# First attention unit loaded in parts, the two heads of a score tile group in turn, and a new order around the start of a fused attention and feed-forward kernel

## The chip, the cores and the metric

The kernel runs on one core of a Trainium2 chip. The metric is the device time of one execution in microseconds (us); the median of several runs is compared. All matrix products run on TensorE (PE), elementwise work on VectorE (DVE) and ScalarE (ACT), a few constants on GpSimd (POOL), and transfers are issued by SyncE (SP) and, in the changed kernel, once by ACT.

## The reference, cut to what matters

```python
def _attn_ref(q, k, v):                       # 4 batches, 8 heads, 576 positions, 64 per head
    scores = scale * np.matmul(q, k.transpose(0, 1, 3, 2))
    mask_local = (rel >= 0) & (rel < 32)                              # heads 0 to 3
    mask_strided = (rel >= 0) & (pos[None, :] % 32 == pos[:, None] % 32)   # heads 4 to 7
    scores = np.where(masks[None], scores, -1e9)
    attn = softmax(scores)                    # exp(s - max) / (sum + 1e-9)
    return np.matmul(attn, v)

x = attn_out as (2304, 512)
x = np.maximum(np.maximum(x @ w1, x @ w2), x @ w3) @ w_out            # 512 -> 768 -> 512
h = x @ w_in                                                          # 512 -> 2048
return (np.maximum(h, 0) + alpha * np.minimum(h, 0)) @ w_out2         # 2048 -> 512
```

Both masks leave only small blocks of the scores: for the local heads 96 queries by 128 keys, for the strided heads (after sorting positions by residue) 108 by 108 or 126 by 126.

## The kernel before

Work on attention comes in units `(b, cc, hf)`: batch `b`, pair of heads `cc` (0 and 1 local, 2 and 3 strided), half `hf`. `ATT_UNITS` gives their order in a batch: (2,0), (2,1), (3,0), (3,1), (0,0), (1,0), (0,1), (1,1). The two heads of a pair lie on partitions 0 to 63 and 64 to 127 of one tile `q` and one tile `k`. A unit has three tiles of each head (two where `cc` is 2 or 3 and `hf` is 1).

For a unit, `scores` (line 325) makes one f32 product per tile and head into two PSUM banks, one per head (tile by tile, head 0 and head 1 in alternation); `masked` (L333, DVE) adds the mask and takes the row extreme; `exponential` (L340, ACT) follows; `reciprocal` (L351, L352) and `normalise` (L364 on DVE or L362 on ACT) come after all of the unit's exponentials; `transposes` (L372, PE) and a copy to `pt` (L264, ACT or DVE) turn each head; `values` (L397, PE) multiplies by v; the result is split into a high and a low part of `x` (L264, L267). Each f32 product shows as two records of PE in the trace.

The feed-forward products of a batch (`L585`, "gates", twelve products of 288 columns for each, and `L607`) need the `x` of all four head pairs of a half, and weights that arrive as 8-byte floats (`raw`, L442), are rebuilt as words by ACT (L456) and DVE (L460, L462) and split into a high part (`w`, L264, ACT) and a low part (L267, DVE).

The order of all this is not written out: each piece is a task with an engine, a cost, and a position `pos`, and `Weave.plan` puts the tasks in order by its own costs, the positions and the rings of buffers. Every engine then runs its list in that order. `first` and `last` set the positions over which a batch's attention is spread; batch 0 stands at -32 to -8, before the first gate at position 0, batch 1 at 16 to 41, among the gates of batch 0. `load_task` issues q and k in one task and v in another, one position later. Two pairs of q and k fit at a time.

`unread` (L214) issues products of 512 columns whose result nobody reads, `WARM` = 6 of them at the start and more as the table `UNREAD` says, so that PE has work while it waits. They read `ident_r`, which POOL makes (L194).

After attention and the first feed-forward part of batches 0 to 2, the last batch and the second feed-forward part follow in an order that the change doesn't touch.

Of the kernel before, what the change touches and what calls it, by code (L numbers as in the profile page):

```python
# [10 lines left out]
F32 = mybir.dt.float32  # L11
F32R = mybir.dt.float32r
# [4 lines left out]
B, H, S, D = 4, 8, 576, 64  # L17
# [4 lines left out]
P = 128  # L22
STRIDE = 32
NA = S // STRIDE
# [6 lines left out]
RG = [(0, 6), (6, 6), (12, 6), (18, 7), (25, 7)]  # L31
# [4 lines left out]
BIG = -8.0e9  # L36
SCALE = 1.0 / math.sqrt(D)
WARM = 6
UNREAD = {((0, 2, 0), 0): 4, ((0, 3, 0), 1): 3, ((0, 1, 0), 0): 9}


NUNITS = 2 * (3 * NF1 + NCC)
NOW = 9
NG = 3 * NF1 // 2
NP = 3
X_SPLIT = 10


class Weave:
# [16 lines left out]
    def add(self, engines, emit, pos, needs=(), gives=(), makes=(), uses=(), mode=None, slack=0):  # L66
        t = len(self.tasks)
        if engines[0][0] != "PE" and any(key in self.banks for key in uses):
            pos -= self.URGENT
        self.banks.update(key for ring, key in makes if ring == "bank")  # L70
        self.tasks.append((engines, emit, pos, needs, makes, mode, slack))
        for ring, key in makes:
            if ring in self.order:
                self.order[ring].append(key)
        for e in gives:
            self.givers.setdefault(e, []).append(t)
            if e[0] == "stored":
                self.stores.add(t)
        for key in [key for _, key in makes] + list(uses):
            self.users.setdefault(key, []).append(t)  # L80
# [84 lines left out]
def attention_maxout_prelu_kernel(  # L165
# [13 lines left out]
    nc = tc.nc  # L179
# [2 lines left out]

    const = ctx.enter_context(tc.tile_pool(name="const", bufs=1, side="left"))
    ident = const.tile([P, P], F32, name="ident")
    ident_r = const.tile([P, P], F32R, name="ident_r")
    mask_l = const.tile([QT, KT], F32, name="mask_l")
    mask_l0 = const.tile([QT, KT], F32, name="mask_l0")
    mask_s = const.tile([P, 126], F32, name="mask_s")
# [1 line left out]

    def build_constants():
        g = nc.gpsimd
        make_identity(nc, ident)
        g.tensor_copy(ident_r, ident)  # L194
        unread(bank(), WARM)
        for m in (mask_l0, mask_l):
            g.memset(m, 0.0)
            g.affine_select(out=m, in_=m, compare_op=ALU.is_ge, fill=BIG, base=32,
                            pattern=[[-1, KT]], channel_multiplier=1)
            g.affine_select(out=m, in_=m, compare_op=ALU.is_ge, fill=BIG, base=-1,  # L200
                            pattern=[[1, KT]], channel_multiplier=-1)
        g.affine_select(out=mask_l0, in_=mask_l0, compare_op=ALU.is_ge, fill=BIG, base=-32,
                        pattern=[[1, KT]], channel_multiplier=0)
        g.memset(mask_s, 0.0)
        ms = mask_s.rearrange("p (r a) -> p r a", a=NA)
        g.affine_select(out=ms, in_=ms, compare_op=ALU.is_ge, fill=BIG, base=0,
                        pattern=[[-NA, 7], [-1, NA]], channel_multiplier=1)
        g.affine_select(out=ms, in_=ms, compare_op=ALU.is_ge, fill=BIG, base=NA - 1,
                        pattern=[[NA, 7], [0, NA]], channel_multiplier=-1)

    def unread(to, n):

        for _ in range(n):
            nc.tensor.matmul(to.rearrange("p (r n) -> p r n", n=P), ident_r,  # L214
                             ident_r.unsqueeze(1).to_broadcast([P, 4, P]), start=True, stop=True)

    def split(hi, lo, src, hi_engine, lo_engine):
        if hi_engine is nc.scalar:
# [26 lines left out]
    qkp = pool(ax, "qkp", 2)  # L245
# [9 lines left out]
    def bank():  # L255
        return ps.tile([P, 512], F32, tag="bank", name="bank")
# [4 lines left out]
    add, tl = weave.add, {}  # L261
# [10 lines left out]
    def dve(n, ops=1):  # L272
        return ("DVE", ops * (75 + 21 * n // 20))

    def load(kb):
        return (("SP", 3 * kb),)
# [13 lines left out]
    def load_task(b, cc, pos):  # L290
        qk, vk = ("q", b, cc), ("v", b, cc)

        def emit_qk(_):
            q = qkp.tile([P, S], F32, tag="q", name="q")
            nc.sync.dma_start(q, qT[b, cc])
            k = qkp.tile([P, S + 32 * (cc < 2)], F32, tag="k", name="k")
            nc.sync.dma_start(k, kTl[b, cc] if cc < 2 else kTs[b, cc - 2])
            tl[qk] = q, k

        def emit_v(_):  # L300
            v = tl[vk] = vp.tile([P, 6 if cc < 2 else 5, 2, D], F32, tag="v", name="v")
            nc.sync.dma_start(v, vl[b, cc] if cc < 2 else vs[b, cc - 2])

        add(load(592), emit_qk, pos, gives=[qk], makes=[("q", qk)])
        add(load(350), emit_v, pos + 1, gives=[vk], makes=[("v", vk)])

    def attention_tasks(b, cc, hf, pos, step):

        u = (b, cc, hf)
        nq, nk, tiles = geometry(cc, hf)  # L310
        n = len(tiles)
        slack = 1500 if b else 0
        ek, qk, vk = ("e", u), ("q", b, cc), ("v", b, cc)
        banks = [("sc", u, j) for j in range(2)]

        def scores(_):
            q, k = tl[qk]
            sc = tl["sc", u] = [bank() for _ in range(2)]
            tl[ek] = ep.tile([P, 2, 3, KT], F32, tag="e", name="e")
            for name in ("nm", "sm", "rc"):  # L320
                tl[name, u] = smp.tile([P, 2, 3], F32, tag=name, name=name)
            for i, (qo, ko, _, _) in enumerate(tiles):
                for j in range(2):
                    rows = slice(D * j, D * (j + 1))
                    nc.tensor.matmul(sc[j][:nq, KT * i:KT * i + nk], q[rows, qo:qo + nq],  # L325
                                     k[rows, ko:ko + nk], start=True, stop=True)

        add((("PE", 2 * n * nk),), scores, pos, needs=[qk], gives=[("sc", u)],
            makes=[("bank", key) for key in banks] + [("e", ek)], uses=[qk], mode="scores")
        for i, (_, _, _, m) in enumerate(tiles):  # L330
            def masked(_, i=i, m=m):
                for j in range(2):
                    nc.vector.tensor_tensor_reduce(  # L333
                        out=tl[ek][:nq, j, i, :nk], in0=tl["sc", u][j][:nq, KT * i:KT * i + nk],
                        in1=m[:nq, :nk], scale=-SCALE, scalar=3.0e38, op0=ALU.add, op1=ALU.min,
                        accum_out=tl["nm", u][:nq, j, i:i + 1])

            def exponential(_, i=i):
                for j in range(2):
                    nc.scalar.activation(tl[ek][:nq, j, i, :nk], tl[ek][:nq, j, i, :nk], AF.Exp,  # L340
                                         bias=tl["nm", u][:nq, j, i:i + 1], scale=-1.0,
                                         accum_out=tl["sm", u][:nq, j, i:i + 1])

            add((dve(nk, 2),), masked, pos, needs=[("sc", u)], gives=[("nm", u, i)],
                uses=banks + [ek])
            add((("ACT", 750),), exponential, pos, needs=[("nm", u, i)], gives=[("exp", u)],
                uses=[ek])

        def reciprocal(_):
# [5 lines left out]
        for j in range(2):  # L355
# [11 lines left out]
            def transposes(_, j=j, trk=trk, ptk=ptk):  # L367
                tr = tl[trk] = bank()
                unread(tr, UNREAD.get((u, j), 0))
                tl[ptk] = ptp.tile([P, 3 * KT], F32, tag="pt", name="pt")  # L370
# [4 lines left out]
            def keep(e, trk=trk, ptk=ptk):  # L375
# [3 lines left out]
                gives=[("nrm", u, j)], uses=[ek])  # L379
            add((("PE", 95 * n),), transposes, pos + step, needs=[("nrm", u, j)], gives=[trk],  # L380
                makes=[("bank", trk), ("pt", ptk)], uses=[ek], mode="transposes", slack=slack)
            add((act(n * nq, True), dve(n * nq)), keep, pos + step, needs=[trk], gives=[ptk],
                uses=[trk, ptk])
# [6 lines left out]
        def values(_):  # L390
# [11 lines left out]
            needs=[vk] + [("pt", u, j) for j in range(2)] + ([begun] if cc >= 2 and hf else []),  # L402
            gives=[pvk] + ([begun] if cc >= 2 and not hf else []), makes=[("bank", pvk)] + [("x", k) for k in fresh],
            uses=[vk] + [("pt", u, j) for j in range(2)] + xks, mode="values", slack=slack)
# [10 lines left out]
        for h in halves:  # L415
# [3 lines left out]
                needs=[pvk], gives=[hik], uses=[pvk])  # L419
# [4 lines left out]
    ATT_UNITS = [(2, 0), (2, 1), (3, 0), (3, 1), (0, 0), (1, 0), (0, 1), (1, 1)]  # L424
# [264 lines left out]
    def last_net(b):  # L689
# [3 lines left out]
        def load_factors(k):  # L693
            if k < NG:
                for i in range(2):
                    t = words["s", k, i] = hw.tile([P, 2, DM], F32R, tag="w", name="w")
                    nc.sync.dma_start(t.bitcast(F32), sd[k - NP][i][:, :, :])
            else:
                n, i = divmod(k - NG, 2)
                load_h(n, ((0, 2), (1, 3))[i])  # L700
# [193 lines left out]
    homes = [("gate", f, g) for f in range(NF1) for g in range(3)] + [("mix", f) for f in range(NF1)]  # L894
    build_constants()
    for b in range(B):
        first, last = (-32, -8) if b == 0 else ((b - 1) * NUNITS + (16 if b == 1 else 3), b * NUNITS - 3)
        step = (last - first) / (len(ATT_UNITS) + 2)
        for i, (cc, hf) in enumerate(ATT_UNITS):
            if i in (0, 2, 4, 5):  # L900
                load_task(b, cc, first + step * i - 8)
            attention_tasks(b, cc, hf, first + step * i, step)
# [35 lines left out]
    for n, _ in enumerate(last_net(B - 1)):  # L938
# [11 lines left out]
        if n == gates - 5:  # L950
            rows = [load_x2(0, 0, xsp, "xs"), load_x2(0, 1, xst, "xst")]
# [329 lines left out]
    for n in range(NQ * NBLK):  # L1281
        blk, q = divmod(n, NQ)
# [68 lines left out]
```

## Time and profile before

| what | value |
|---|---|
| median of 3 runs | 747.61 us (747.39 to 748.48) |
| the profiled execution | 746.98 us, of which the span of the trace is 745.2 us |
| PE, DVE, ACT busy | 99%, 86%, 62% of the span |
| TensorE clock granted, mean of the span | 0.998 of full speed |

The span runs from the first to the last instruction of the core; 1.8 us of the execution lie around it. Busy shares are means over the whole span, so the start, where attention of batch 0 has no feed-forward work beside it, has to be read apart from the rest.

### The profile page before, as it was taken

Reading aid. Unit: us, or ns where it says so; the run is one execution under the profiler, and the core shown is the slowest. Engines: PE = TensorE matmul, PEld = TensorE weight load, DVE = VectorE, ACT = ScalarE, POOL = GpSimd, SP = SyncE. Lnnn points to the kernel's source line nnn. Section 1 sums busy time; section 2 is a strip of 40 time slices with the busy share of each in tenths; the row PEclk is TensorE's granted clock in tenths of the full one; section 3 lists DMA queues with packets and bytes.
Section 4 is the critical chain, followed back from the end, with each engine's and each line's share of the span. In section 5 each row is a group of like instructions: output and inputs, shape, how many; then the busy total and the mean of one; then the engine's idle time right before and its main releaser. Section 6 shows DMA issues by size and latency. Waiting matters only on the chain.

```text
span 745.2 us, 16023 instructions
## 1 busy us (share of the span) xinstructions
PE 734.8 (99%) x5570; PEld 710.9 (95%) x5570; DVE 640.1 (86%) x1711; ACT 462.8 (62%) x1254; POOL 28.8 (4%) x42
## 2 busy tenths in 40 slices
PE   7899999999999999999999999999999999999998
PEld 5699999999999999999999999999999999999997
DVE  5999999899988999487769898888989888988896
ACT  7987889568674888332255656625575654556571
POOL 1000000000000000034500000000000000000000
PEclk9999999999999999999999999999999999999999
DMA  8577769996999765779899789999789999877362
GB/s 270 169 239 223 229 217 330 373 334 240 312 307 340 264 234 194 258 283 337 297 322 376 267 301 330 383 399 385 248 302 305 360 401 363 295 242 256 114 200 77
DMA packets 88929, 211.96 MB, mean 284 GB/s; under 512 B 11024, under 2 KB 41232, under 8 KB 88848
## 3 DMA queue, kind: packets, MB, share of 16 engines
q1 hardware_dynamic: 88848, 210.94, 81.4%
q8 instruction: 44, 0.72, 0.4%
q14 instruction: 37, 0.30, 0.1%
HBM read 154.80 MB, written 56.10 MB: 283 GB/s over the span
## 4 chain that ended last, share of the span: by engine, by line
PE 87%; ACT 4%; DMA 3%; DVE 2%; POOL 2%; issue 1%; SPq 0%; POOLq 0%; ACTq 0%; DVEq 0%
PE bank L585 26%; PE ph L1190 22%; PE po L991 15%; PE bank L607 8%; PE po L997 4%; PE ph L991 3%; PE bank L325 2%; PE bank L397 2%; PE bank L372 2%; PE po L1001 2%; ACT e L340 2%; DMA xd<-xst 1%; POOL xst L222 1%; DMA xs<-x 1%; DMA xst<-x 1%
## 5 line engine op out<-in xcount | busy, mean ns | idle before, releaser
L1190 PE MATMUL ph<-x,w 128*128 128x384 f32 x990 | 200.2, 337 | 0.2 <-DVE c L1196 0.2
L585 PE MATMUL bank<-x,w 128*128 128x288 f32 x1440 | 197.5, 297 | 0.0
L585 PEld LDWEIGHTS bank<-x,w 128*128 128x128 f32 x1440 | 191.8, 189 | 2.0
L1190 PEld LDWEIGHTS ph<-x,w 128*128 128x128 f32 x990 | 166.3, 188 | 1.4 <-DVE c L1196 0.6
L991 PE MATMUL po<-w,g 128*128 128x256 f32 x936 | 135.6, 281 | 0.0
L991 PEld LDWEIGHTS po<-w,g 128*128 128x128 f32 x936 | 130.2, 189 | 0.3
L1196 DVE TENSOR_TENSOR c<-ph,c 128x384 f32<-128x384 f32 x165 | 89.4, 554 | 30.8 <-PE ph L1190 27.4
L984 ACT CAST g<-c 128x384 fp32r<-128x384 f32 x93 | 47.0, 505 | 91.0 <-DVE c L1174 51.8
L607 PE MATMUL bank<-h,w 128*128 128x288 f32 x576 | 79.4, 297 | 0.0
L607 PEld LDWEIGHTS bank<-h,w 128*128 128x128 f32 x576 | 76.9, 189 | 0.9
L264 ACT CAST w<-word 128x512 fp32r<-128x512 f32 x100 | 57.9, 591 | 23.4 <-DMA wp<-w 7.7
L340 ACT ACTIVATE e<-e,nm 96x128 f32<-96x128 f32 (+2 forms) x176 | 68.4, 403 | 5.4 <-DVE nm L333 5.3
L267 DVE TENSOR_TENSOR w<-word,w 128x512 fp32r<-128x512 f32 x100 | 63.3, 641 | 9.6 <-ACT w L264 9.3
L1134 ACT ACTIVATE c<-c 128x384 f32<-128x384 f32 x96 | 50.5, 526 | 32.8 <-DVE c L1196 31.8
L1135 ACT ACTIVATE c<-c,nalpha 128x384 f32<-128x384 f32 x96 | 59.2, 617 | 3.1
L1139 DVE SCALAR_TENSOR_TENSOR c<-c 128x384 f32<-128x384 f32 x96 | 53.0, 552 | 6.4 <-ACT c L1135 6.4
L985 DVE TENSOR_TENSOR g<-c,g 128x384 fp32r<-128x384 f32 x96 | 52.9, 551 | 0.9 <-ACT g L984 0.5
L456 ACT ACTIVATE word<-raw 128x512 f32<-128x512 f32 x56 | 37.7, 683 | 16.3 <-DMA raw<-in_w 12.0
L985 DVE TENSOR_TENSOR g<-k,g 128x384 fp32r<-128x384 f32 x72 | 37.0, 551 | 7.5 <-ACT g L984 7.5
L997 PE MATMUL po<-w,g 128*128 128x512 f32 x120 | 43.0, 398 | 0.0
L462 DVE SCALAR_TENSOR_TENSOR word<-raw,word 128x512 uint32<-128x512 uint32 x56 | 38.8, 692 | 1.9
L1174 DVE TENSOR_TENSOR k<-c 128x384 f32<-128x384 f32 x72 | 37.9, 550 | 0.0
(107 smaller groups left out, 942.1 us busy)
## 6 DMA issues: line engine op xcount, KB each, us to landing
w<-wh SPq DMA_DIRECT2D x72, 512.0 KB, 5.2
raw<-in_w SPq DMA_DIRECT2D x50, 512.0 KB, 5.0
w<-wo SPq DMA_DIRECT2D x48, 512.0 KB, 5.7
w<-wp SPq DMA_DIRECT2D x36, 512.0 KB, 6.4
wh<-w SPq DMA_DIRECT2D x24, 512.0 KB, 4.6
xd<-xst SPq DMA_DIRECT2D x28, 384.0 KB, 3.1
x<-xd SPq DMA_DIRECT2D x28, 384.0 KB, 8.4
ws<-w SPq DMA_DIRECT2D x12, 512.0 KB, 5.3
```

Source lines behind the costliest of these rows:

```text
L264: (nc.scalar.copy if e == "ACT" else nc.vector.tensor_copy)(out_, in_)
L267: nc.vector.tensor_tensor(out=out_, in0=x, in1=y, op=ALU.subtract)
L340: nc.scalar.activation(tl[ek][:nq, j, i, :nk], tl[ek][:nq, j, i, :nk], AF.Exp, bias=tl["nm", u][:nq, j, i:i + 1], scale=-1.0, accum_out=tl ...
L585: nc.tensor.matmul(acc, words["gate", f, g][:, wi, cc * P:(cc + 1) * P], xt[b, cc, hf][:, xi, :], start=n == 0, stop=n == 3 * NCC - 1)
L607: nc.tensor.matmul(acc, words["mix", f][:, wi, dc * P:(dc + 1) * P], st["h", hf, f][:, xi, :], start=n == 0, stop=n == 3 * NF1 - 1)
L985: return g, lambda: nc.vector.tensor_tensor(out=g[:, 1], in0=x, in1=g[:, 0].bitcast(F32), op=ALU.subtract)
L991: nc.tensor.matmul(bank[:, NH * half:NH * (half + 1)], g[:, gi, t * P:(t + 1) * P], w[:, wi, off:off + NH], start=first and i == 0, stop=l ...
L997: nc.tensor.matmul(bank.rearrange("p (s n) -> p s n", n=NH), g[:, 0, t * P:(t + 1) * P], w[:, :, off:off + NH], start=first, stop=last)
L1135: nc.scalar.activation(a, a, AF.Copy, scale=nalpha[:, f:f + 1])
L1139: nc.vector.scalar_tensor_tensor(out=a, in0=h, scalar=0.0, in1=a, op0=ALU.max, op1=ALU.add)
L1190: nc.tensor.matmul(bank, words["h", n, i][:, wi, off + c * P:off + (c + 1) * P], x2h[blk, k, c][:, xi, :], start=m == 0, stop=m == 5)
L1196: nc.vector.tensor_tensor(out=out_, in0=bank, in1=other, op=ALU.add)
```

## The change

The change has these parts.

- The first unit's q and k come in two transfers each: columns 0 to 323 (three tiles, `PART`) first, k's from ACT's queue and q's from SP's, then the rest (`emit_rest`); the second unit of that load, (2,1), waits for the rest as well. The v of the first load moves from one position behind to 5.5 positions behind.
- `scores` loops over heads first and tiles second, and `masked` and `exponential` take their six pieces in that order, two at a time (`pieces`).
- The unread products read `warm_r`, which DVE sets to 1.0, instead of `ident_r`; POOL makes no `ident_r`. `UNREAD` has eight instead of four ahead of the first transposes. A line that lets `scores` issue unread products is there too, but the table has no entry for it.
- Batch 1's attention begins at position 12 instead of 16.

```diff
-UNREAD = {((0, 2, 0), 0): 4, ((0, 3, 0), 1): 3, ((0, 1, 0), 0): 9}
+UNREAD = {((0, 2, 0), 0): 8, ((0, 3, 0), 1): 3, ((0, 1, 0), 0): 9}
+PART = NA * (RG[2][0] + RG[2][1])
...
-        make_identity(nc, ident)
-        g.tensor_copy(ident_r, ident)
-        unread(bank(), WARM)
+        nc.vector.memset(warm_r.bitcast(F32), 1.0)
+        unread(bank(), WARM)
+        make_identity(nc, ident)
...
+            if parted:
+                nc.scalar.dma_start(k[:, :PART], kTs[b, cc - 2, :, :PART])
+                nc.sync.dma_start(q[:, :PART], qT[b, cc, :, :PART])
+            else:
+                nc.sync.dma_start(q, qT[b, cc])
+                nc.sync.dma_start(k, kTl[b, cc] if cc < 2 else kTs[b, cc - 2])
+
+        def emit_rest(_):
+            q, k = tl[qk]
+            nc.sync.dma_start(q[:, PART:], qT[b, cc, :, PART:])
+            nc.sync.dma_start(k[:, PART:], kTs[b, cc - 2, :, PART:])
...
-        add(load(592), emit_qk, pos, gives=[qk], makes=[("q", qk)])
-        add(load(350), emit_v, pos + 1, gives=[vk], makes=[("v", vk)])
+        parted = (b, cc) == (0, ATT_UNITS[0][0])
+        kb = 592 * PART // S if parted else 592
+        add(load(kb), emit_qk, pos, gives=[qk], makes=[("q", qk)])
+        if parted:
+            add(load(592 - kb), emit_rest, pos + 1, gives=[("rest", *qk)], uses=[qk])
+        add(load(350), emit_v, pos + (5.5 if parted else 1), gives=[vk], makes=[("v", vk)])
...
-            for i, (qo, ko, _, _) in enumerate(tiles):
-                for j in range(2):
-                    rows = slice(D * j, D * (j + 1))
+            for j in range(2):
+                rows = slice(D * j, D * (j + 1))
+                for i, (qo, ko, _, _) in enumerate(tiles):
                     nc.tensor.matmul(sc[j][:nq, KT * i:KT * i + nk], q[rows, qo:qo + nq],
                                      k[rows, ko:ko + nk], start=True, stop=True)
...
-        for i, (_, _, _, m) in enumerate(tiles):
-            def masked(_, i=i, m=m):
-                for j in range(2):
+        pieces = [(j, i) for j in range(2) for i in range(n)]
+        for k in range(n):
+            def masked(_, k=k):
+                for j, i in pieces[2 * k:2 * k + 2]:
+                    m = tiles[i][3]
...
-        first, last = (-32, -8) if b == 0 else ((b - 1) * NUNITS + (16 if b == 1 else 3), b * NUNITS - 3)
+        first, last = (-32, -8) if b == 0 else ((b - 1) * NUNITS + (12 if b == 1 else 3), b * NUNITS - 3)
```

The plan orders all tasks anew, so instructions move where no line of the diff names them. Three places matter.

PE at the end of batch 0's attention, before (from the scores of (1,1) on; L325 scores, L372 transposes, L397 values, L585 gates):

```order
L325 MATMUL bank<-k,q 96x128 x6
L397 MATMUL bank<-pt,v 64x96 x6
L214 MATMUL bank<-ident_r 128x512 x9
L372 MATMUL bank<-ident,e 128x96 x6
L325 MATMUL bank<-k,q 108x108 x6
L397 MATMUL bank<-pt,v 64x96 x6
L372 MATMUL bank<-ident,e 128x96 x6
L325 MATMUL bank<-k,q 126x126 x4
L397 MATMUL bank<-pt,v 64x96 x6
L372 MATMUL bank<-ident,e 128x96 x6
L325 MATMUL bank<-k,q 108x108 x6
L585 MATMUL bank<-x,w 128x288 x240
```

The same place now (L339 scores, L389 transposes, L414 values, L602 gates):

```order
L389 MATMUL bank<-ident,e 128x96 x6
L414 MATMUL bank<-pt,v 64x96 x6
L339 MATMUL bank<-k,q 108x108 x6
L414 MATMUL bank<-pt,v 64x96 x6
L602 MATMUL bank<-x,w 128x288 x12
L389 MATMUL bank<-ident,e 128x96 x6
L339 MATMUL bank<-k,q 126x126 x4
L414 MATMUL bank<-pt,v 64x96 x6
L389 MATMUL bank<-ident,e 128x96 x6
L602 MATMUL bank<-x,w 128x288 x12
L414 MATMUL bank<-pt,v 64x96 x6
L602 MATMUL bank<-x,w 128x288 x168
```

Two gates of twelve products now stand among the last units of batch 0, and one group of batch 1's scores (108x108) has moved behind the first long run of gates.

ACT's first rows before (L340 exponentials, L264 copies of the transposed heads and high parts of x):

```order
L340 ACT_TABLE_LOAD
L340 ACTIVATE e,sm<-e,nm 108x108 x6
L340 ACTIVATE e,sm<-e,nm 126x126 x4
L340 ACTIVATE e,sm<-e,nm 108x108 x4
L264 COPY pt<-bank 108x324 x2
L340 ACTIVATE e,sm<-e,nm 108x108 x2
L264 COPY pt<-bank 126x252 x2
L340 ACTIVATE e,sm<-e,nm 126x126 x2
L264 CAST x<-bank 128x9x18 x2
```

And now (L357 exponentials, L265 copies, L473 words of a weight, L379 normalising):

```order
L298 DMA k<-in_kTs 128x324
L357 ACT_TABLE_LOAD
L357 ACTIVATE e,sm<-e,nm 108x108 x6
L357 ACTIVATE e,sm<-e,nm 126x126 x4
L357 ACTIVATE e,sm<-e,nm 108x108 x4
L265 COPY pt<-bank 108x324
L357 ACTIVATE e,sm<-e,nm 108x108 x2
L473 ACTIVATE word<-raw 128x512
L265 COPY pt<-bank 126x252
L357 ACTIVATE e,sm<-e,nm 126x126 x2
L265 CAST x<-bank 128x9x18 x2
L379 ACTIVATE e<-e,rc 108x108 x3
```

One of the two copies of each strided unit has gone (to DVE), and the words of the first weight and a normalising have come in early.

SP's first rows now (L299 and L306 the two parts of q, L307 the rest of k, L301 and L302 q and k of the second load, L311 v); before, a v followed each of the first two pairs of q and k:

```order
L299 DMA q<-in_qT 128x324
L306 DMA q<-in_qT 128x252
L307 DMA k<-in_kTs 128x252
L301 DMA q<-in_qT 128x576
L302 DMA k<-in_kTs 128x576
L311 DMA v<-in_vs 128x640 x2
```

Both v's of the strided pairs now stand behind the second pair's q and k.

## Rows read from the trace of the kernel before

**Rows 1.** Busy time in two stretches; us, busy and count of instructions of PE

```profile
36.00:745.00 709.00, 705.64 (x5296) 1.00 0.83 288
```

**Rows 2.** The same view over the start, all engines: PE, PEld, DVE, ACT, POOL, clock, DMA

```profile
0.00:36.00 36.00, 29.14 (x277) 21.69 (x278) 26.55 (x158) 30.71 (x136) 3.51 (x17) 0.95 0.68 221
36.00:80.00 44.00, 44.00 (x356) 43.14 (x354) 42.00 (x101) 35.46 (x97) 0.00 (x0) 1.00 0.73 222
...
12.00:36.00 24.00, 20.91 (x232) 15.74 (x230) 21.51 (x120) 24.00 (x107) 0.00 (x0) 1.00 0.62 199
```

**Rows 3.** Chain of work that ended last, first 40 us: start, length, what

```profile
1.38 0.29 POOL ident_r L194
1.72 2.93 PE bank L214 x6
...
6.07 4.96 ACT e L340 x26
...
34.05 0.75 PE bank L325 x12
...
35.68 4.33 PE bank L585 x31
```

**Rows 4.** PE in order of time, first 8 us: start, length; idle before, releaser

```profile
4.57 1.48 PE L325 MATMUL bank<-k,q 64*108 64x108 f32 x20
7.93 0.35 PE L325 MATMUL bank<-k,q 64*108 64x108 f32 x2 [1.88 <-DMA k<-in_kTs]
```

**Rows 5.** Clock granted around that wait; columns as in rows 2

```profile
8.00:10.00 2.00, 2.00 (x15) 1.62 (x16) 1.11 (x11) 2.00 (x12) 0.00 (x0) 0.61 1.06 352
```

**Rows 6.** ACT in order of time: start, length, line, shape

```profile
16.05 0.45 ACT L264 COPY pt<-bank 108x324 f32<-108x324 f32 x1
16.38 0.40 ACT L340 ACTIVATE e<-e,nm 96x128 f32<-96x128 f32 x1
16.77 0.39 ACT L340 ACTIVATE e<-e,nm 96x128 f32<-96x128 f32 x1
...
19.00 1.26 ACT L456 ACTIVATE word<-raw 128x512 f32<-128x512 f32 x2
20.15 0.63 ACT L264 COPY pt<-bank 126x252 f32<-126x252 f32 x2
20.66 0.42 ACT L340 ACTIVATE e<-e,nm 96x128 f32<-96x128 f32 x1
...
29.43 1.04 ACT L362 ACTIVATE e<-e,rc 96x128 f32<-96x128 f32 x3
30.32 0.66 ACT L264 CAST w<-word 128x512 fp32r<-128x512 f32 x1
30.83 0.44 ACT L264 CAST x<-bank 128x288 fp32r<-128x288 f32 x1
...
33.60 0.72 ACT L456 ACTIVATE word<-raw 128x512 f32<-128x512 f32 x1
```

**Rows 7.** Chain of work among the gates: scores, transposes, values, gates

```profile
80.14 8.15 PE bank L585 x60
...
99.80 1.14 PE bank L372 x12
...
206.90 0.75 PE bank L325 x12
207.65 1.14 PE bank L397 x24
```

**Rows 8.** Scores alone in two stretches of 10 ns: PE busy, PEld busy (records running)

```profile
4.57:4.58 0.01, 0.01 (x1) 0.01 (x2) 1.00 0.64 256
4.58:4.59 0.01, 0.01 (x2) 0.01 (x2) 1.00 0.64 231
```

**Rows 9.** Transfers of the first 40 us: issues by tile, KB each, median us to landing; raw alone

```profile
q<-in_qT SPq DMA_DIRECT2D x7, 288.0 KB, 3.2
...
DMA to landing us min/median/max: 3.6/4.9/7.5
```

More of the change, by code (lines that the diff above doesn't have):

```diff
@@ L184, in attention_maxout_prelu_kernel @@
     ident = const.tile([P, P], F32, name="ident")
-    ident_r = const.tile([P, P], F32R, name="ident_r")
+    warm_r = const.tile([P, P], F32R, name="warm_r")
     mask_l = const.tile([QT, KT], F32, name="mask_l")
@@ L213, in unread @@
         for _ in range(n):
-            nc.tensor.matmul(to.rearrange("p (r n) -> p r n", n=P), ident_r,
-                             ident_r.unsqueeze(1).to_broadcast([P, 4, P]), start=True, stop=True)
+            nc.tensor.matmul(to.rearrange("p (r n) -> p r n", n=P), warm_r,
+                             warm_r.unsqueeze(1).to_broadcast([P, 4, P]), start=True, stop=True)
     def split(hi, lo, src, hi_engine, lo_engine):
@@ L293, in emit_qk @@
         def emit_qk(_):
[L294 to L298, printed above, removed]
+            q, k = tl[qk] = (qkp.tile([P, S], F32, tag="q", name="q"),
+                             qkp.tile([P, S + 32 * (cc < 2)], F32, tag="k", name="k"))
+            if parted:
[8 more added lines that the diff above has]
+            nc.sync.dma_start(k[:, PART:], kTs[b, cc - 2, :, PART:])
         def emit_v(_):
@@ L318, in scores @@
             sc = tl["sc", u] = [bank() for _ in range(2)]
+            unread(sc[0], UNREAD.get(u, 0))
             tl[ek] = ep.tile([P, 2, 3, KT], F32, tag="e", name="e")
@@ L321, in scores @@
                 tl[name, u] = smp.tile([P, 2, 3], F32, tag=name, name=name)
-            for i, (qo, ko, _, _) in enumerate(tiles):
-                for j in range(2):
-                    rows = slice(D * j, D * (j + 1))
+            for j in range(2):
+                rows = slice(D * j, D * (j + 1))
+                for i, (qo, ko, _, _) in enumerate(tiles):
                     nc.tensor.matmul(sc[j][:nq, KT * i:KT * i + nk], q[rows, qo:qo + nq],
                                      k[rows, ko:ko + nk], start=True, stop=True)
-        add((("PE", 2 * n * nk),), scores, pos, needs=[qk], gives=[("sc", u)],
+        whole = [("rest", *qk)] if (b, cc) == (0, ATT_UNITS[0][0]) and hf else []
+        add((("PE", 2 * n * nk),), scores, pos, needs=[qk] + whole, gives=[("sc", u)],
             makes=[("bank", key) for key in banks] + [("e", ek)], uses=[qk], mode="scores")
-        for i, (_, _, _, m) in enumerate(tiles):
-            def masked(_, i=i, m=m):
-                for j in range(2):
+        pieces = [(j, i) for j in range(2) for i in range(n)]
[3 more added lines that the diff above has]
+                    m = tiles[i][3]
                     nc.vector.tensor_tensor_reduce(
@@ L336, in masked, with exponential @@
                         accum_out=tl["nm", u][:nq, j, i:i + 1])
-            def exponential(_, i=i):
-                for j in range(2):
+            def exponential(_, k=k):
+                for j, i in pieces[2 * k:2 * k + 2]:
                     nc.scalar.activation(tl[ek][:nq, j, i, :nk], tl[ek][:nq, j, i, :nk], AF.Exp,
@@ L342, in exponential @@
                                          accum_out=tl["sm", u][:nq, j, i:i + 1])
-            add((dve(nk, 2),), masked, pos, needs=[("sc", u)], gives=[("nm", u, i)],
+            add((dve(nk, 2),), masked, pos, needs=[("sc", u)], gives=[("nm", u, k)],
                 uses=banks + [ek])
-            add((("ACT", 750),), exponential, pos, needs=[("nm", u, i)], gives=[("exp", u)],
+            add((("ACT", 750),), exponential, pos, needs=[("nm", u, k)], gives=[("exp", u)],
                 uses=[ek])
```

## The prediction

> **What bounds the kernel now.** I read the busy times by stretch first. From 36 us to the end PE is busy 705.64 of 709.00 us [rows 1]: there the time is PE's work, and a change of order among other engines shows only if it makes PE wait. The first 36 us are different [rows 2]: PE is busy 29.14 us, and part of that is unread products. So the next view is the chain of work that ended last, over the first 40 us. It goes from `ident_r` on POOL (done at 1.67 us) through six unread products (2.93 us) to the first scores, and from 6.07 us on mostly through ACT [rows 3]. ACT is busy all 24.00 us from 12 to 36 us [rows 2], and the long run of gates begins at 35.68 us [rows 3]. The start is a queue of ACT work with a few us of waiting ahead of it; behind it PE decides.
>
> [...]
>
> **The change part by part.**
>
> *Earlier beginning.* A memset on DVE replaces `ident`, the select and `ident_r` on POOL. The trace has no such memset; the nearest row is the 0.29 us cast [rows 3]. Engines are released at about 0.74 us, so unread products can begin at about 1.0 instead of 1.72. Six take 2.93 us, so PE is free for scores at 3.9; it began them at 4.57 [rows 4]. Would the data be there? Whole q's took 3.2 us from issue to landing [rows 9]; the parts have 162 of 288 KB, are issued side by side, and land at 0.74 + 3.2 = 3.9 at the latest. Bounds: if the landing decides and is no faster than the 4.57 of before, 0; if both are quicker, 0.9. I take **0.65 us** earlier, first exponential at 5.4. ACT's own transfer is issued ahead of the table load, which has 3 us of room.
>
> *v behind the second pair.* 320 KB fewer stand ahead of the second q and k. The wait of 1.88 us should shrink by about 1. On ACT, which has fourteen exponentials to do in that time (26 records in 4.96 us [rows 3], so 0.37 us each), the wait cost little: it shows as some 0.5 us of ACT idle near 11.7 us, while the first transposes run at the low clock. I take that **0.5 us** back; 0 if the clock still falls. v itself is not wanted until the first values, after 12 us. [...]
>
> *ACT's list.* Counted on the order up to the last copy of batch 0's heads (it ended before at 33.60 us [rows 6]), with the spacings between starts in the rows of ACT [rows 6]:
>
> - copies: two of 108x324 (0.33 each), two of 126x252 (0.26) fewer, one of 128x288 (0.29) more: -0.9
> - normalising on ACT: before one of three tiles (29.43 to 30.32, 0.89); now three of three and one of two (0.6, estimate from two thirds): +2.4
> - words of weights: five instead of three (1.15 for two): +1.15
> - high parts of weights: three instead of one (0.51 each): +1.0; and a gate's copy: +0.3
>
> Together +3.95 us. So the last copy ends at 33.60 - 0.65 - 0.5 + 3.95 = 36.4, and the last normalising, with 1.6 us of rows behind it in the list, at 34.8. On PE follow the last transposes and the last values (0.57 each: 1.14 for two units' worth [rows 7]), with a gate of twelve between them (60 products in 8.15 us, 1.63 [rows 7]). The long run begins at 34.8 + 0.57 + 1.63 + 0.57 = **37.5**, later than before. But two gates are then done, 3.26 us; before, at 37.5, PE had done 1.82 us of the long run and 0.75 us of batch 1's scores [rows 3]. Balance: 3.26 - 1.82 - 0.75 = **0.7 us gained**.
>
> *DVE* takes three more copies, two or three more words (two steps each) and two more low parts, and gives up three normalisings: about +2.5 us (an estimate, with some 0.6 us a step, as ACT takes for the same 128x512 shape, and 0.45 a copy [rows 6]). In 36 us it is busy 26.55 [rows 2] and starts only at about 5.75, so it has 3.7 us idle. It fits, with little over. If it doesn't, the later weights are late and gates wait: DVE is at 42.00 of 44 from 36 to 80 us. I put the bounds of the balance at -1.5 (waits between the two full lists) and +2.7 (the 2.15 us of words and high parts of weights turn out to lie off the path).
>
> *Batch 1 four positions ahead.* It spreads the same work over more gates. Cost 0: covered by PE's gates, bound as above.
>
> *Heads in turn.* No instruction is added; the question is whether the two heads still run beside each other. The second score record starts within 10 ns of the first [rows 8]. Either it is the other head, on the other half of the rows, and has then passed the first product's own second record; or the two records of one product run together. Six products (twelve records) take 0.75 us [rows 7], so 0.125 us for each two records. In the first reading PE starts a waiting record although one ahead of it is held; now it has to do so past five held records instead of one. In the second the order of heads is of no account. Ends: 0, and everything in a row. For the latter, a three-tile unit goes from six steps to ten (the second head can start beside the first's last tile), a two-tile unit from four to six; batches 1 to 3 have 18 and 6 of them: 18 x 4 + 6 x 2 = 84 steps x 0.125 = +10.5 us, all on PE where PE is the bound. I take 0, the nearer to the row, where a record did start beside another at once [rows 8].
>
> [...]
>
> **Sum.** The profiled execution took 746.98 us; -0.7 gives 746.3. It lies 0.6 under the median of the runs shown, 747.61, which would give 746.9. I say **746.6**.
>
> **How it could go otherwise.** What a measurement can tell here is about 0.2%, 1.5 us.
>
> 1. *The forecast*, 745.0 to 748.0: 50%. Of it 15 faster, 32 same, 3 slower.
> 2. *The start gives more*, -2.7 us, 744.5: 22%. The weights' words and casts on ACT turn out to fill waits, and the earlier scores keep the clock up. For it: the 1.88 us wait and the clock at 0.61 are gone together. Against: ACT had no idle time after 12 us.
> 3. *Heads one after the other*, +10.5 - 0.7, about 757: 14%. For it: the order of code puts five records of one head ahead of the other's first. Against: the records that start together [rows 8].
> 4. *Half of that*: PE looks a tile or two ahead, so that a three-tile unit gains two steps: 18 x 2 x 0.125 = 4.5, less 0.7, about 751: 7%.
> 5. *ACT waits for a raw weight.* The words of the first weight now stand ahead of most of the exponentials on ACT, at 5.4 + 14 x 0.37 + 0.33 + 2 x 0.37 = 11.7 us. SP issues the raw at about 6.3; 4.9 us to landing gives 11.2, the slowest 7.5 gives 13.8 [rows 9], and every exponential behind waits with it. Landing after 12.4 eats the gain; at 13.8 the kernel is 1.4 us slower, 748.5: 7%, near the edge of what can be told.
>
> That the change does nothing is inside the first case: the parts may land early and wait for the unread products.
>
> **Numbers.** Faster: 15 + 22 = 37%. Same: 32%. Slower: 3 + 14 + 7 + 7 = 31%. The range takes in cases 1, 2, 4 and 5 and leaves case 3 and a tail below: 744.0 to 753.0. Case 1's own range is 745.0 to 748.0.
>
> **What would show it.** First exponential at about 5.4 us instead of 6.07, and PE's second wait at about 1 us. The clock at 1.0 from 8 to 12 us (case 2), or still low. ACT without a gap at its first word, else case 5. The long run of gates at about 37.5 us with two gates ahead of it. Six products of scores among later gates in 0.75 us, and five or six records running at once; if they take 1.2 us or more with two or three running, case 3 holds and the prediction is wrong by ten us. PE busy without a gap after 38 us; gaps there, with DVE as releaser, would say that the weights were late.

## The result, and the profile after

The changed kernel takes 758.74 us (median of 6 runs, 755.60 to 761.76); the kernel before, beside it, 747.41 (747.19 to 748.48). The ratio is 1.0141, 95% interval 1.0117 to 1.0165: 10.5 us slower (0.0141 x 747.4), where 746.6 was forecast. A ratio here is not the quotient of the two medians beside it (that would be 1.0152), so a loss worked out from a ratio differs from the difference of the medians. The profiled execution took 757.27 us, of which 755.2 are span.

First the busy times of the changed kernel by stretch (PE, PEld, DVE, ACT, POOL, clock, DMA):

```profile
0.00:36.00 36.00, 30.61 (x234) 23.32 (x234) 24.03 (x145) 26.81 (x116) 3.22 (x16) 0.95 0.65 213
36.00:80.00 44.00, 42.75 (x352) 40.54 (x352) 41.17 (x105) 37.80 (x109) 0.00 (x0) 1.00 0.69 210
12.00:36.00 24.00, 20.24 (x174) 15.38 (x172) 17.98 (x103) 19.40 (x84) 0.00 (x0) 0.93 0.58 195
```

Against [rows 2], ACT is busy 19.40 of the 24 us from 12 to 36 us, where it was full. PE is busier than before in the first 36 us (30.61 against 29.14) and has fewer records done (234 against 277): part of its work runs more slowly, as the next rows show. The chain of work that ended last over the first 60 us, with the rows behind 11 us cut to those used:

```profile
0.84 0.18 DVE warm_r L194
1.06 2.93 PE bank L215 x6
3.98 2.73 PE bank L339 x20
6.73 0.33 SPq L301
7.10 0.43 SPq L302
7.57 6.19 DMA raw<-in_w
...
25.50 0.48 DVE e L381
25.98 0.04 issue
26.02 0.47 PE bank L389 x3
26.49 1.65 PE bank L339 x12
28.13 3.33 PE bank L215 x9
31.46 0.50 PE bank L389 x6
...
40.75 1.65 PE bank L602 x12
...
43.05 16.99 PE bank L602 x127
```

The start is not the queue of ACT work of [rows 3] any more. It goes through twenty records of scores in 2.73 us (1.48 in [rows 4]), a raw weight that lands at 13.8 us, a normalising of DVE for which PE waits until 26.0 us, and unread products at 0.37 us each. The long run of gates begins at 43.05 us instead of 35.68. Who waits for whom says the same; first PE, from 15 to 40 us, then ACT, from 10 to 36 us (us in total, times, longest):

```profile
PE bank L389 <- DVE e L381: 2.9, 2, 1.8
PE bank L389 <- ACT e L379: 1.9, 2, 1.1
```

```profile
ACT pt L265 <- PE bank L389: 2.9, 1, 2.9
ACT word L473 <- DMA raw<-in_w: 1.4, 1, 1.4
```

Behind the start, the chain from 60 to 110 us shows scores among gates:

```profile
72.12 1.03 PE bank L339 x12
...
78.68 0.64 PE bank L339 x8
...
84.28 1.12 PE bank L339 x12
```

Twelve records took 0.75 us in [rows 7], which is a strided unit; here a strided unit takes 1.03 and a local one 1.12. A unit of two tiles (eight records) takes 0.64.

### The profile page after: what moved, and what is told of

It reads as the page before. It is cut to its first block, busy times and chain, and to the rows that moved or that the text cites. A ratio compares the mean times of both kernels' runs of the same rounds, so it can differ in the third digit from the quotient of the medians.

```text
span 755.2 us, 16035 instructions
## 1 busy us (share of the span) xinstructions
PE 744.8 (99%) x5574; PEld 719.3 (95%) x5574; DVE 641.5 (85%) x1708; ACT 465.3 (62%) x1257; POOL 28.2 (4%) x41
## 4 chain that ended last, share of the span: by engine, by line
PE 89%; DMA 4%; ACT 3%; POOL 2%; issue 1%; DVE 1%; SPq 0%; ACTq 0%; POOLq 0%; DVEq 0%
PE bank L602 26%; PE ph L1207 23%; PE po L1008 15%; PE bank L624 8%; PE po L1014 4%; PE bank L339 4%; PE ph L1008 3%; PE bank L414 2%; PE bank L389 2%; PE po L1018 2%; DMA xs<-x 2%; POOL xst L223 1%; ACT e L357 1%; PE bank L215 1%; DMA raw<-in_w 1%
## 5 line engine op out<-in xcount | busy, mean ns | idle before, releaser
L602 PE MATMUL bank<-x,w 128*128 128x288 f32 x1440 | 199.2, 297 | 0.0
L602 PEld LDWEIGHTS bank<-x,w 128*128 128x128 f32 x1440 | 192.0, 188 | 2.6 <-issue 0.2
L357 ACT ACTIVATE e<-e,nm 96x128 f32<-96x128 f32 (+2 forms) x176 | 68.3, 400 | 7.7 <-DVE nm L350 7.5
L265 ACT CAST w<-word 128x512 fp32r<-128x512 f32 x100 | 57.6, 588 | 20.3 <-DMA wh<-w 6.0
L473 ACT ACTIVATE word<-raw 128x512 f32<-128x512 f32 x56 | 37.6, 681 | 12.7 <-DMA raw<-in_w 6.8
```

What stands on the lines that cost most here:

```text
L265: (nc.scalar.copy if e == "ACT" else nc.vector.tensor_copy)(out_, in_)
L602: nc.tensor.matmul(acc, words["gate", f, g][:, wi, cc * P:(cc + 1) * P], xt[b, cc, hf][:, xi, :], start=n == 0, stop=n == 3 * NCC - 1)
```

## The experiments

Theory H: the heads in turn cost PE time, because a record of the other head can no longer run beside the one that is held. Theory O: the new order of the lists costs it, by waits at the start. The first four kernels tell them apart.

**e1_alternate**: 751.29 us, ratio to before 1.0059 [1.0039, 1.0079]. The changed kernel with only this:

```diff
-for j in range(2): ...
-    for i, (qo, ko, _, _) in enumerate(tiles):
+for i, (qo, ko, _, _) in enumerate(tiles):
+    for j in range(2): ...
```

> The changed kernel with only the products of scores back in alternation (tile by tile, head 0 and head 1); the order of every list stays that of the changed kernel. Theory H (heads in turn cost time on PE, because a head's products wait behind five of the other's): the scores from 36 us on take 24.1 us of PE in the changed kernel and 17.4 before, so 6.7 us come back there and 1 to 2 more in batch 0, time about 750. Theory O (the new order of the lists costs the time: ACT waits for a raw weight, the long run of gates begins late): no more than 2 us come back, 757 or more. Both in part: 750 leaves some 3 us for O.

Both in part: 0.82% or 6.1 us come back (1.0141 to 1.0059), 4.4 us stay. Its chain from 60 to 110 us has the three kinds of unit at

```profile
73.41 0.75 PE bank L339 x12
79.70 0.64 PE bank L339 x8
85.32 0.83 PE bank L339 x12
```

So heads in turn cost 0.28 to 0.29 us for a unit of three tiles, and nothing for one of two.

**e2_heads_in_turn**: 751.77 us, 1.0065 [1.0041, 1.0089]. The reverse edit in the kernel before.

> The kernel before with only the products of scores heads first, tiles second; all else as before. Theory H: 6.7 us more in batches 1 to 3 and 1 to 2 in batch 0, time 755 to 756. Theory O: within 1.5 us of 747.4.

4.9 us by the ratio, less than forecast and far over O. The groups of scores on PE from 45 to 320 us, in the kernel before and in this one (count, busy us, mean ns):

```profile
L325 PE MATMUL bank<-k,q 64*96 64x128 f32 (+2 forms) x232 | 17.4, 281 | 0.0
```

```profile
L325 PE MATMUL bank<-k,q 64*96 64x128 f32 (+2 forms) x232 | 21.5, 281 | 0.0
```

No record is longer (281 ns), but fewer run beside each other: 4.1 us. The changed kernel and e1_alternate have in the same stretch

```profile
L339 PE MATMUL bank<-k,q 64*96 64x128 f32 (+2 forms) x244 | 23.4, 281 | 0.0
```

```profile
L339 PE MATMUL bank<-k,q 64*96 64x128 f32 (+2 forms) x244 | 18.4, 281 | 0.0
```

which is 5.0 us. By units: 17 of the 18 three-tile units of batches 1 to 3 lie in that stretch here, 17 x 0.29 = 4.9.

**e3_position_12** (the kernel before, `16` to `12`): 749.82 us, 1.0027 [1.0011, 1.0043]. **e4_alternate_16** (e1_alternate, `12` to `16`): 754.56 us, 1.0093 [1.0065, 1.0120].

> The kernel before with only batch 1's attention begun at position 12 instead of 16. Theory O, if the position is what costs: 749 to 752, with gaps of PE behind 36 us. Theory H: 746.5 to 748.5.

> The changed kernel with the products of scores in alternation and batch 1 at position 16. What then is left of the change is the load in parts, v later, the memset and four more unread products. If these cost the rest (ACT waits for its first raw weight until 13.8 us, the long run begins 5 to 7 us later than before): as e1_alternate, about 750. If position 12 costs the rest: 746 to 747.

The position alone costs some 2 us in the old list, but taking it back in the new one does not help. What it costs depends on the list around it, so it gets no share of its own here.

**e5_blocks_of_two**: 748.11 us, 1.0010 [0.9996, 1.0024]. The kernel before with

```diff
-for i, (qo, ko, _, _) in enumerate(tiles):
-    for j in range(2): ...
+for i, j in [(0, 0), (1, 0), (0, 1), (1, 1), (2, 0), (2, 1)][:2 * n]: ...
```

> The kernel before with the products of scores in blocks: tiles 0 and 1 of head 0, tiles 0 and 1 of head 1, then tile 2 of both. Theory H in its sharper form (PE starts a waiting head past at most two products of the other head, since the two-tile units take the same 0.6 to 0.64 us in both orders while three tiles go from 0.75 to 1.12): six products among gates still take 0.75 to 0.8 us, time 747 to 748.5. The rival (every step away from alternation costs in proportion): 0.9 us or more for six, time 749 to 750.

The sharper form holds; the proportional rival falls. Scores busy from 45 to 320 us, as before:

```profile
L325 PE MATMUL bank<-k,q 64*96 64x128 f32 (+2 forms) x232 | 17.4, 281 | 0.0
```

The starts of the twelve records of one local unit, from the trace in us behind the first, show past how many held records PE started one of the other head. a1 to a6 are head 0's records and b1 to b6 head 1's, in program order. Which is which is read from marks: the first record of each head takes 347 or 348 ns and the rest 269, and the last of a head raises a semaphore.

```
e5_blocks_of_two  a1 0, b1 .013, a2 .187, b2 .201, a3 .296, b3 .310, a4 .406, b4 .419, ... last .636
changed kernel    a1 0, a2 .188, a3 .297, b1 .303, a4 .406, b2 .489, a5 .515, b3 .599, a6 .624, b4 .708, b5 .817, b6 .926
```

In blocks of two, b1 starts with a2, a3 and a4 held ahead of it. With the heads in turn it does not start while five or four are held (a1 and a2 running) and starts 6 ns after a3, when three are left. It does not go by the time from a1 on: in the first unit of the changed kernel, whose records are longer (384 ns, where these take 269), a3 starts at 0.489 us behind a1 and b1 at 0.495. Nor does a semaphore hold it in that unit: neither b1 nor the weight load ahead of it waits for one in the trace. In the changed kernel's unit of two tiles at 78.6 us, with a2, a3 and a4 held ahead, b1 starts 0.013 us behind a1, as in blocks of two. In the local unit, once b1 has begun, three pairs run side by side, and the last three records of head 1 alone: nine steps instead of six. Three steps of 0.109 us are 0.33, less what overlaps at the ends. Windows of 10 ns agree (PE busy, records running); the changed kernel has two while head 1 is held, four when it has begun, six for a moment at 84.83 us, and two at the end:

```profile
84.45:84.46 0.01, 0.01 (x2) 0.01 (x2) 0.00 (x0) 0.01 (x1) 0.00 (x0) 1.00 0.99 410
84.54:84.55 0.01, 0.01 (x4) 0.01 (x3) 0.00 (x0) 0.01 (x1) 0.00 (x0) 1.00 0.76 307
85.25:85.26 0.01, 0.01 (x2) 0.00 (x0) 0.00 (x0) 0.01 (x2) 0.00 (x0) 1.00 0.58 230
```

**e6_raw_first**: 751.29 us, 1.0045 [1.0025, 1.0064]. **e7_unread_4**: 752.32 us, 1.0052 [1.0038, 1.0067]. **e8_whole_load**: 749.07 us, 1.0014 [0.9999, 1.0028]. Each is e1_alternate with one edit: the task that fetches the first raw weight moved, in the finished order, ahead of the third pair's q and k; and

```diff
-UNREAD = {((0, 2, 0), 0): 8, ...
+UNREAD = {((0, 2, 0), 0): 4, ...          # e7
-parted = (b, cc) == (0, ATT_UNITS[0][0])
+parted = False                            # e8, and no wait of (2,1) for the rest
```

> The changed kernel with scores in alternation, and the first raw weight issued ahead of the third pair's q and k instead of behind them (which wait for the second unit's scores); nothing else moves. If ACT's wait for that raw (until 13.8 us, some 1.9 us of ACT) lies on the path: 1 to 2 us under e1_alternate, 749.5 to 750. If PE's pauses and the clock behind them decide instead: as e1_alternate, 751.3, within 1.

> The changed kernel with scores in alternation and four instead of eight unread products ahead of the first transposes. If the four more cost PE time at the head of the queue (1 us at the upper level, 2 at the lower): 1 to 2 us under e1_alternate, about 750. If they keep the clock up and fill a pause: as e1_alternate or slower.

> The changed kernel with scores in alternation, and the first load as before: q and k whole and from SP, v one position behind. The list order then is nearly that of e3_position_12 (749.8). If the load in parts (with the list that it brings) is what is left of the loss: 748 to 750. If it is a gain by itself (scores from 4.0 us): 752 or more.

In e6 the wait for the raw weight is gone, and ACT is full from 12 to 24 us:

```profile
12.00:24.00 12.00, 9.58 (x104) 6.48 (x101) 10.95 (x65) 12.00 (x54) 0.00 (x0) 1.00 0.59 207
```

yet the median is that of e1_alternate, and the ratios cannot be told apart: 1.0 us in the middle, with intervals that allow from nothing to some 3 us. Nor is the comparison a clean one: no raw weight stands in e1_alternate's own chain, where the first transposes begin at 13.50 us; in the changed kernel they begin at 10.29. The four unread products cost nothing that can be told either: in the changed kernel the eight take 2.11 us from 8.25 us on at a granted clock of 1.00, 0.26 each, and the first five from 28.06 us on take 2.46 us, 0.49 each; the clock from 28 to 30 us is 0.50. The load as before takes back 0.45% (1.0059 to 1.0014), some 3.4 us, and here the intervals lie apart. It takes back the load in parts and the later v together; no run tells the two apart.

**e9_whole_same_list**: 754.98 us, 1.0082 [1.0057, 1.0106]. e1_alternate with the order of all lists kept, but the first task transfers q and k whole and the second nothing.

> The changed kernel with scores in alternation and with the order of all lists kept as the load in parts made it, but the first q and k transferred whole from SP (nothing in the second task). If the loss that the load in parts brings (e1_alternate against e8_whole_load, 2.2 us) comes from the list's order, by PE's wait of 1.9 to 2.2 us at the transposes near 26 us: about 751, with that wait there. If it comes from the transfers themselves: about 749, without it.

With the transfers whole again nothing comes back, so what is left is the list, though the time lies 4 us over the forecast and nothing here explains that. PE's wait near 27 us is there:

```profile
27.46 0.47 PE L387 MATMUL bank<-ident,e 96*128 96x96 f32 x3 [1.89 <-DVE e L379]
```

**e10_turn_in_batch_0**: 750.91 us, 1.0024 [1.0004, 1.0043]. **e15_turn_in_batches_1_3**: 752.77 us, 1.0060 [1.0042, 1.0078]. The kernel before, with the six pairs (head, tile) listed head by head and sorted by tile again where the heads are to alternate:

```diff
+pairs = [(j, i) for j in range(2) for i in range(n)]
+if b:                                     # e10; "if not b" in e15
+    pairs.sort(key=lambda p: p[1])
```

> The kernel before with the heads in turn in batch 0 alone. Theory H: PE's 2.7 us more of scores in the first 45 us stand beside ACT's full list and cost little: 747.5 to 749, so that the 3.9 us of e2_heads_in_turn are those of batches 1 to 3. Rival: the start is as dear as the rest, 750 or more.

> The kernel before with the heads in turn in batches 1 to 3 alone. Theory H: PE is the bound there, so its 4.2 us more of scores behind 45 us (as in e2_heads_in_turn) are 4 us of the time: 751.5 to 753. Rival (the loss is at the start): within 1.5 us of the kernel before.

Batches 1 to 3 cost 4.5 us, as forecast, where PE is full. Batch 0 costs 0.3 to 3.2 us by its interval, 1.8 in the middle. The median lies over the range that H gave it and in the rival's, and the middle is what its six three-tile units would cost at 0.29 each: that ACT's list covers the cost at the start is not borne out. The two together, 0.84%, agree with e2_heads_in_turn's 0.65% within the intervals.

**e11_memset_fill**: 748.75 us, 1.0004 [0.9989, 1.0018]. **e12_memset**: 750.05 us, 1.0006 [0.9988, 1.0024]. The kernel before with the memset (e12), and besides it (e11)

```diff
+UNREAD = {(0, 3, 0): 8, ...               # and the line in scores that reads it
```

> The kernel before with the memset for the unread products, and eight more of them ahead of the third unit's scores, where PE waited 1.88 us for the second pair's k and then fell to the lower clock. If the pause causes the fall and the fall costs time at the start: the clock stays at 1.0 from 8 to 12 us and the time is 0.5 to 2 us under the kernel before. If ACT's list hides it: the same within 1 us.

> The kernel before with only the memset for the unread products instead of the select and copy of POOL. PE can begin 0.66 us earlier (1.06 instead of 1.72). If the start shifts with it: 0.3 to 0.7 us faster, hard to tell. If the transfers decide when scores begin, or the longer pause behind them costs clock: the same, or up to 2 us slower.

Neither can be told from the kernel before. In e12 PE begins at 1.06 us, yet the scores begin at 4.57 as in [rows 4], now waiting for k, and take longer. In e11 the eight products are too many for the pause and run slowly, so that the third scores begin at 10.43 instead of 7.93; PE in order of time, e12 first:

```profile
4.57 2.30 PE L325 MATMUL bank<-k,q 64*108 64x108 f32 x20 [0.59 <-DMA k<-in_kTs]
8.12 1.42 PE L325 MATMUL bank<-k,q 64*108 64x108 f32 x12 [1.25 <-DMA k<-in_kTs]
```

```profile
6.72 3.78 PE L214 MATMUL bank<-warm_r 128*128 128x512 f32 x8
10.43 0.82 PE L326 MATMUL bank<-k,q 64*108 64x108 f32 x12
```

**e13_normalise_first**: 750.67 us, 1.0031 [1.0015, 1.0047]. e1_alternate with one task of the finished order moved: DVE's normalising of head 1 of unit (0,0,0) right behind that of head 0.

> The changed kernel with scores in alternation, and one task moved: DVE normalises head 1 of unit (0,0,0) right behind head 0, ahead of the masked tiles and the low parts of x that stood between. Theory L (what is left of the loss is the new list: PE's transposes of that head wait 1.9 to 2.2 us near 26 us for this normalising, and the next scores, which ACT needs, wait behind them): PE's wait there falls under 0.7 us and the time 1 to 2.5 us under e1_alternate (751.3). If the wait is covered by ACT's full list anyway: as e1_alternate.

PE's wait near 26 us is gone; PE in order of time:

```profile
23.36 0.65 PE L420 MATMUL bank<-pt,v 126*64 126x126 f32 x8
23.94 0.71 PE L395 MATMUL bank<-ident,e 96*128 96x96 f32 x6
24.59 0.90 PE L345 MATMUL bank<-k,q 64*96 64x128 f32 x12
```

ACT is busy 22.77 us from 12 to 36 us, against 18.75 in e1_alternate and 22.81 in e8_whole_load:

```profile
12.00:36.00 24.00, 21.17 (x203) 15.34 (x201) 21.66 (x113) 22.77 (x95) 0.00 (x0) 0.98 0.64 202
```

0.28% comes back, 2.1 us, inside the forecast; but the intervals of the two kernels overlap. Nor does ACT's busy time single this wait out: in e6_raw_first, where PE waits 2.14 us at the same place, ACT is busy 22.93 of the 24 us. So this wait is a candidate for the rest and not a proven source.

**e14_after_blocks**: 752.61 us, 1.0061 [1.0038, 1.0084]. The changed kernel with the loop of e5_blocks_of_two.

> The changed kernel with the products of scores in blocks: tiles 0 and 1 of head 0, tiles 0 and 1 of head 1, then tile 2 of both; nothing else changed. If PE starts a waiting head past two held products but not past three, in this kernel as in the kernel before: as e1_alternate, 750 to 752, and six products among gates in 0.75 to 0.85 us. If not: 754 or more.

As e1_alternate by the ratio, the median 0.6 over the forecast; scores busy from 45 to 320 us against 18.4 and 23.4:

```profile
L339 PE MATMUL bank<-k,q 64*96 64x128 f32 (+2 forms) x244 | 18.6, 281 | 0.0
```

No kernel here is faster than the one before.

## Why the prediction was wrong

**The step that failed first: "Heads in turn ... I take 0".** The question was put rightly, with its evidence ("past five held records instead of one"), and the answer was taken from a row that showed PE passing one held record. Three held records were passed, not five (b1 0.013 us behind a1 in e5_blocks_of_two, 0.303 us in the changed kernel). The price is that of the fourth case, not of the third: three steps for a three-tile unit and none for a two-tile one (put there at two steps, 4.5 us). The forecast for it was 7%. It measured 5.0 us in PE's rows, 4.5 us in the time of e15_turn_in_batches_1_3, and with batch 0 the 6.1 us that e1_alternate takes back. That the whole loss equals the 10.5 us of the third case is coincidence.

The records of the two heads did not start in program order: b1 starts 0.212 us ahead of a5, the first record of head 0's third product, in the changed kernel, and 0.283 us ahead of a3, of its second product, in e5_blocks_of_two, which cost nothing that can be told (1.0010 [0.9996, 1.0024]).

**The second: "ACT's list", and with it the 37.5 us.** I counted what each engine has to do and let the lists run without waiting, since ACT had not waited before. The list that the load in parts brings does make it wait: PE reaches the transposes of unit (0,0,0) before DVE has normalised its second head; the next scores and nine unread products stand behind, on PE's own queue; and ACT waits 2.92 us for the transposes behind those. The long run begins at 43.05, not 37.5. Before, at 43.05, the long run was 7.37 us old and one more group of batch 1's scores was done (0.75 us); now two gates (3.3 us) are done instead: 4.8 us lost where 0.7 were to be gained. The clock has a part in it: behind PE's wait, at a granted clock of 0.73 and 0.50, the nine unread products take 3.40 us, and 2.34 in e6_raw_first, where the clock is 1.00 behind a wait of 2.14 us. Executions with nearly the same lists differ: the long run begins at 44.34 us in e1_alternate's profile (753.77 us) and at 40.01 in e6_raw_first's (750.38). By the ratios, e1_alternate against e8_whole_load gives 3.4 us of the same kind, and e9_whole_same_list says that it is not the transfers. Which of the waits carries it stays open. The bound of that balance, -1.5 for "waits between the two full lists", was too narrow.

**The sum**: 6.1 for the heads in turn, 3.4 for the list of the load in parts, and 1.0 for all the rest, which e8_whole_load cannot tell from nothing (0.9999 to 1.0028). The two profiled executions agree: 5.0 us of scores behind 45 us and 4.8 at the start are 9.8 of the 10.0 us between their spans (755.2 and 745.2).

**Earlier beginning.** Right in its first half: the memset ends at 1.02, the unread products begin at 1.06, the scores at 3.97 (forecast 3.9). Then twenty records took 2.70 us instead of 1.48, and the first exponential came at 5.86, not 5.4. The step took the duration of scores from before. PE in order of time:

```profile
1.06 2.93 PE L215 MATMUL bank<-warm_r 128*128 128x512 f32 x6 [1.06 <-DVE warm_r L194]
3.97 2.70 PE L339 MATMUL bank<-k,q 64*108 64x108 f32 x20
7.25 1.07 PE L339 MATMUL bank<-k,q 64*108 64x108 f32 x12 [0.58 <-DMA k<-in_kTs]
```

In e12_memset twenty records in alternation took 2.30 us, and in e13_normalise_first, which alternates too and starts its scores at 3.92, twelve took 1.42 us and the next eight 0.95, so most of the lengthening does not come from the order of heads.

**v behind the second pair.** Right in the profiled execution, in part by luck: the wait is 0.58 us instead of 1.88 [rows 4] (about 1 was forecast), and the clock granted from 8 to 10 us is 1.00 instead of 0.61 [rows 5], from 10 to 12 us 1.00 instead of 0.53. The second pair's k lets PE go on at 7.25 instead of 7.93; the other half of the gain is that the slow scores end later. With the same transfers PE goes on at 8.37 in e1_alternate, where the clock of the first 12 us is 0.83; in e13_normalise_first it waits 1.71 us, until 8.19, and the clock from 8 to 12 us is 0.69. Nor does the clock stay at 1.00 in the changed kernel: it is 0.73 from 26 to 28 us and 0.50 from 28 to 30 us, right behind the 1.85 us wait, though from 24 to 36 us it is 1.00 in e6_raw_first, with a wait of 2.14 us, and in e9_whole_same_list, with one of 1.89 us:

```profile
26.00:28.00 2.00, 1.98 (x15) 1.65 (x15) 1.97 (x6) 2.00 (x12) 0.00 (x0) 0.73 0.62 247
28.00:30.00 2.00, 2.00 (x6) 1.55 (x6) 1.97 (x13) 0.83 (x3) 0.00 (x0) 0.50 0.38 88
```

**ACT waits for a raw weight** (the fifth case). It came as described: landed at 13.8 us, the slow end, and ACT stood 1.42 us. But e6_raw_first, without it, is no faster that can be told, so no run here shows that its 1.4 us were part of the price.

**Batch 1 four positions ahead**: cost 0 was taken. Alone it costs about 2 us (1.0027 [1.0011, 1.0043]); within the change its share stays open. Open too is what makes e4_alternate_16 and e9_whole_same_list slower than e1_alternate, if they are: the intervals overlap.

## What to carry to other kernels

Where small products of two row halves are to run side by side, the order of code sets how many records stand between a product and its partner; two f32 products ahead were free here (0.83 us for a local unit, as in alternation) and three were not (1.12 us), so alternate, or count. When a planner makes a new order, do not add up the work of an engine that was full: ask for each list which instruction waits first, and what else stands behind it on the same engine. And price an edit apart in each stretch: here the batches where PE is full gave back what PE's rows say (4.1 us there, 4.5 measured), while at the start the measurement leaves 0.3 to 3.2 us open.

## What the runs showed of the hardware that was not expected

PE started a record of the other row half past three held records (b1 0.013 us behind a1 in e5_blocks_of_two) and not past four (0.303 us in the changed kernel, once three are left); nothing in the kernel before showed this.

At the start the column of the granted clock does not account for the length of PE's records. It reads 1.00 from 0 to 8 us in the changed kernel, while the six unread products ahead take 0.49 us each and those from 8.25 us take 0.26. The trace of the changed kernel holds no record of the clock ahead of 6.46 us, that of the kernel before none ahead of 5.04, so the clock of those products is not shown. The profiles differ in when the records become short, though the unread products ahead were the same six: twenty records of scores took 1.48 us in the kernel before and 2.30 in e12_memset, where PE had begun 0.66 us earlier and then waited 0.59 us. That may be part of why an earlier beginning gave nothing; no run here isolates it.
